# One more pair of block 1's first product by seven half-size products, and its weight sums spread over VectorE and adding transfers

## The chip, the cores and the metric

The kernel runs on one NeuronCore of a Trainium2 chip. The metric is the device time of one execution in microseconds (us). Engines are named as the profile names them: PE (TensorE, matmuls), DVE (VectorE), ACT (ScalarE), POOL (GpSimd) and SP (SyncE, which here only issues transfers).

## The reference

```python
for t in range(S):                        # retention; q, k, v are (4, 8, 768, 64)
    state = gamma * state + k[t] outer v[t]
    y[:, :, t] = scale * q[:, :, t] @ state
x = y.transpose(0, 2, 1, 3).reshape(3072, 512)
h = x @ w_in                              # 512 x 2048
g = h * (1.0 / (1.0 + np.exp(-1.702 * h)))
out = (g @ w_out).astype(np.float32)      # 2048 x 512
```

## The kernel before

**Tiling.** The recurrence is computed in chunks of 64 steps for two batches at once; four chunks make a block of 512 rows of x, and there are six blocks. A block's first product is x @ w_in with the gate after it, its second g @ w_out. The hidden dimension has 16 column tiles of 128; `p` numbers eight groups of two tiles, and a *pair* `d` (0 to 3) is the groups 2d and 2d+1. The four weight quadrants of group p lie in slots 0 to 3 of `W1A` (p below 4) or `W1B` (p from 4 on). Both weight matrices come as 64-bit floats and are narrowed on the chip: `w{n}a`, `w{n}b` fetch the raw words by SP's queue, `abs{n}` is one ACT pass over 128x1024 (line 207), `half{n}` three DVE passes (lines 211 to 213), `rest{n}` three more (lines 217 to 222). n from 0 to 7 are the groups of w_in, 8 to 15 the tiles of w_out. There are three raw buffers; the fetch of n waits for `rest` of n-3.

**The order.** Until the second products begin, a list of names, written out by hand (lines 929 to 945), sets the order. Every step named there is emitted in turn; a step wrapped in `pin` keeps its place among its engine's pinned instructions, and PE's own order is always that of emission. DVE, ACT, POOL and SP then take their instructions in that order. What isn't pinned (until the change: POOL's `decay` and `aged` from chunk 6 on, lines 274 and 359) may be placed elsewhere by a planner.

**Block 1's first product.** Pair 2 is computed the plain way: `up1.8` to `up1.11` (line 427), each four matmuls 128x512 into one PSUM bank, which the gate (`hidden`, line 393) reads. Pairs 0, 1 and 3 each use seven products instead of eight (`seven{d}.0` to `seven{d}.6`): each product is four matmuls 128x256, whose operands are quadrants or sums of quadrants. In this text k0 to k6 are those seven. With w the weight quadrants (slots 0 to 3) and x the four quadrants of block 1 (`X1`), the sums are

- w4 = w2 + w3, w5 = w4 - w0, w6 = w0 - w2, and a last one, w1 - w5, which the old code calls 2;
- x4 = X1[2] - X1[0], x5 = X1[3] - x4, x6 = X1[3] - X1[2], x2 = X1[1] - x5, four DVE passes in `seven_x`.

k0, k2, k4 and one later product accumulate in one PSUM bank of tag `x`; three times a running value is copied out by ACT (`kept`, line 479: p1 after k0, u after k2, vv after k4), and the next product into that bank can't start until the copy has read it. The other products go to banks of tag `y`, which DVE reads in `tensor_add` (lines 488, 494, 498, 499). Each tag has two banks. The outputs are a0 to a3 of `G`, each then gated in place by ACT, a1 straight from PSUM. `p1` and `t` share one SBUF buffer, `u` and `vv` have one each.

**The weight sums before.** For each of the three pairs `seven_w{d}` makes three ACT copies with a sign (line 450) and three transfers from POOL's queue that add to their destination (line 452); w5's waits for w4's. `seven_v{d}` adds one copy (line 459) and one transfer (line 460). The buffers are those that later chunks use as qT, at, o (two each) and kT (one).

After the list come the second products: `down(0)` uses block 0's activations and the narrowed w_out, all of which (`rest15` last) must be there for its seventh unit; its own weight sums are `sums_w2` (lines 521 to 523, DVE), and `sums_g` (lines 530 to 532, DVE) rewrites block 0's activations while `down(0)` runs.

Of the kernel before, what the change touches and what calls it, by code (L numbers as in the profile page):

```python
# [9 lines left out]
F32 = mybir.dt.float32  # L10
U32 = mybir.dt.uint32
AF = mybir.ActivationFunctionType
ALU = mybir.AluOpType
P = 128
# [14 lines left out]
def kernel(  # L29
# [29 lines left out]
    pe, act, dve, pool, sp = nc.tensor, nc.scalar, nc.vector, nc.gpsimd, nc.sync  # L59
    ctx.enter_context(tc.manual_schedule(engines={mybir.EngineType.PE}))  # L60

    B, H, S, D = q.shape
    NT, DM = out.shape
    DFF = moe_w_in.shape[1]
    HP = H // 2
# [13 lines left out]
    one = ctx.enter_context(tc.tile_pool(name="one", bufs=1))  # L79
    two = ctx.enter_context(tc.tile_pool(name="two", bufs=2))  # L80
# [23 lines left out]
    cold = const.tile([P, 2 * H], F32, name="cold")  # L104
    whole = const.tile([P, HP], F32, name="whole")
    whole_h = const.tile([P, H], F32, name="whole_h")
# [5 lines left out]
    def w1(p):  # L112

        return (W1A, p) if p < NP // 2 else (W1B[p // 2 - 2], p % 2)
# [3 lines left out]
    def pin(i):  # L118
        return tc.keep_in_program_order(i) if ordered[0] else i
# [107 lines left out]
    QT, KT, KD, AT, TURNED, PA, PU, PY, SHARE = [{} for _ in range(9)]  # L227
# [35 lines left out]
    def decay(j):  # L263

        if j % NC == NC - 1:
            return
        KD[j] = home(j, "kd")
        x = QKV["kn", j]
        if j < NEW:

            for h in range(H):
                pin(act.activation(KD[j][:, h], x[:, h % HP * 2 + h // HP], AF.Copy, scale=cold[:, H + h:H + h + 1]))
        else:
            pool.tensor_mul(KD[j].rearrange("p (i s) d -> p i s d", i=2), x.rearrange("p (i s) d -> p i s d", i=2),
                            cold[:, None, H:H + HP, None].to_broadcast([P, 2, HP, D]))

    def by_half(t, j):

# [72 lines left out]
    def aged(f):  # L351

        c = f % NC
        old, new = state[c % 2], state[(c + 1) % 2]
        if f < NEW:
            for s in range(HP):
                pin(act.activation(new[:, :, s], old[:, :, s], AF.Copy, scale=whole[:, s:s + 1]))
        else:
            pool.tensor_mul(new.rearrange("p r s d -> p (r s) d"), old.rearrange("p r s d -> p (r s) d"),
                            whole_h[:, :, None].to_broadcast([P, H, D]))  # L360

    def updated(f):
        c = f % NC
# [26 lines left out]
    def hidden(g, h):  # L390

        for g, i in g if isinstance(g, list) else [(g, slice(0, 2))]:
            pin(act.activation(g, h[:, i], AF.Gelu_apprx_sigmoid))  # L393
# [37 lines left out]
    SUM_X, SUM_W = {}, {}  # L431

    def seven_x():
# [3 lines left out]
        for to, a, b in ((SUM_X[4], X1[:, 2], X1[:, 0]), (SUM_X[5], X1[:, 3], SUM_X[4]),  # L437
                         (SUM_X[6], X1[:, 3], X1[:, 2]), (SUM_X[2], X1[:, 1], SUM_X[5])):
            pin(dve.tensor_sub(to, a, b))

    def seven_w(d):

        t, q1 = w1(2 * d)
        w = [t[:, q1:q1 + 2, s].rearrange("p u c f -> p u (c f)") for s in range(4)]
        SUM_W[d] = {4: one.tile([P, 2, 2 * P], F32, name="w4", tag="qT", bufs=2),
                    5: one.tile([P, 2, 2 * P], F32, name="w5", tag="at", bufs=2),
                    6: two.tile([P, 2, 2 * P], F32, name="w6", tag="o")}
        m = SUM_W[d]
        for to, of, sign in ((4, 2, 1.0), (6, 2, -1.0), (5, 0, -1.0)):
            pin(act.activation(m[to], w[of], AF.Copy, scale=sign))  # L450
        for to, of in ((m[4], w[3]), (m[6], w[0]), (m[5], m[4])):
            pin(pool.dma_start(to, of, accum_op=ALU.add))

    def seven_v(d):

        t, q1 = w1(2 * d)
        m = SUM_W[d]
        m[2] = one.tile([P, 2, 2 * P], F32, name="w2", tag="kT")
        pin(act.activation(m[2], m[5], AF.Copy, scale=-1.0))
        pin(pool.dma_start(m[2], t[:, q1:q1 + 2, 1].rearrange("p u c f -> p u (c f)"), accum_op=ALU.add))  # L460

    SEVEN = {}

    def seven(d, k):

        t, q1 = w1(2 * d)
        a = [G[:, 2 * d:2 * d + 2, s, :] for s in range(4)]

        def product(acc, sa, sb, start, stop):
            for u in range(2):  # L470
                for c in range(2):
                    w = SUM_W[d][sa][:, u, c * P:(c + 1) * P] if sa in (4, 5, 6, 2) else t[:, q1 + u, sa, c, :]
                    x = SUM_X[sb][:, c, :] if sb in SUM_X else X1[:, sb, c, :]
                    pe.matmul(acc[:, u, :], w, x, start=(start and u == 0 and c == 0), stop=(stop and c == 1),  # L474
                              skip_group_check=True)

        def kept(name, tag, src):
            SEVEN[name] = one.tile([P, 2, TH], F32, name=name, tag=tag)
            pin(act.activation(SEVEN[name], src, AF.Copy))

        if k in (0, 1, 3, 5):
            SEVEN["x" if k == 0 else f"y{k}"] = ps.tile([P, 2, TH], F32, name="ph", tag="x" if k == 0 else "y")
        acc = SEVEN[f"y{k}" if k in (1, 3, 5) else "x"]
        product(acc, (0, 1, 5, 4, 6, 2, 3)[k], (0, 1, 5, 4, 6, 3, 2)[k], k in (0, 1, 3, 5), k in (1, 3, 5, 6))
        if k == 0:
            kept("p1", "s1", acc)
        elif k == 1:
            pin(dve.tensor_add(a[0], acc, SEVEN["p1"]))
        elif k == 2:
            kept("u", "s2", acc)  # L490
            hidden(a[0], a[0])
        elif k == 3:
            SEVEN["t"] = one.tile([P, 2, TH], F32, name="t", tag="s1")
            pin(dve.tensor_add(SEVEN["t"], acc, SEVEN["u"]))
        elif k == 4:
            kept("vv", "s3", acc)
        elif k == 5:
            pin(dve.tensor_add(a[3], SEVEN["y3"], SEVEN["vv"]))
            pin(dve.tensor_add(a[2], acc, SEVEN["t"]))
        else:  # L500
            for s in (3, 2):
                hidden(a[s], a[s])
            hidden(a[1], acc)

    def sums_w1(p):
        t, q1 = w1(p)
# [318 lines left out]
    works, products = {}, {}  # L825
# [72 lines left out]
        works[f"step-{j}"] = lambda j=j: attend(None, j)  # L898
    works["seven_x"] = seven_x
    for d in range(NP // 2):  # L900
        works |= {f"seven_w{d}": lambda d=d: seven_w(d), f"seven_v{d}": lambda d=d: seven_v(d)}
        for n in range(7):
            works[f"seven{d}.{n}"] = lambda d=d, n=n: seven(d, n)
    for i in range(2 * NFF):
        works[f"w{i // 2}{'ab'[i % 2]}"] = lambda i=i: fetch(i)
    for name, i in [("0a", 0), ("0b", 1)] + [(str(p), 2 * p) for p in range(1, NFF)]:
        n = Narrow(i)
# [20 lines left out]
    for name in """  # L928
        k0 table q0 warm turn0 w0b rows warm k1 abs0b q1 turned0 step0 v0 w0a half0b mask k2 turn1 causal rest0b
        masked0 decay0 v1 decay1 abs0a half0a step-0 updated0 turned1 q2 step1 rowd whole w2b turn2 w2a x0 k3  # L930
        aged1 masked1 turned2 v2 rest0a abs2 q3 step-1 updated1 state1 decay2 aged2 step2 q4 x1 half2 decay3 w3b
        w3a up0.0.0 masked2 turn3 k4 step-2 v3 q5 rest2 k5 gate0.0.0 turned3 updated2 state2 step3 up0.0.2
        masked3 abs3 half3 x2 rest3 turn4 w1b step-3 aged3 gate0.0.2 turned4 state3 w1a w5b updated3 v5 decay4
        abs1 x3 turn5 half1 up0.0.3 turned5 up0.1.2 step4 aged4 w5a rest1 v4 gate0.0.3 decay5 w6a masked4
        gate0.1.2 abs5 w6b step5-4 half5 rest5 up0.0.1 updated4 abs6 state4 gate0.0.1 w4b
        up0.1.1 half6 aged5 w4a up0.0.5 rest6 masked5 up0.1.5 gate0.1.1 x4 gate0.0.5 abs4 step-5 w8b w8a
        half4 gate0.1.5 state5 updated5 anew q6 up0.1.6 x5 rest4 gate0.1.6 abs8 v6 up0.0.6 w7b w7a half8
        turn6 gate0.0.6 up0.1.0 abs7 half7 gate0.1.0 w9b w9a up0.1.4 q7 gate0.1.4 decay6 step6 masked6 rest7 up0.0.4 v7
        gate0.0.4 turn7 up0.1.3 gate0.1.3 aged6 step7-6 masked7 updated6 decay7 abs9 state6 x6 up0.0.7 rest8 gate0.0.7
        w11a w11b step-7 state7 x7 seven_w0 half9 w10b w10a up0.1.7 rest9 gate0.1.7 seven_x abs11 half11  # L940
        up1.8 gate1.8 seven_v0 w12a w12b rest11 up1.9 gate1.9 abs10 seven_w1 half10 up1.10 gate1.10 w14b w14a rest10
        up1.11 abs12 gate1.11 seven0.0 seven0.1 half12 w13a w13b seven0.2 seven0.3 rest12 abs14 seven0.4 seven0.5
        half14 seven0.6 aged7 seven_v1 w15a w15b qk8 seven1.0 seven1.1 abs13 rest14 seven1.2 seven1.3 updated7 half13
        seven_w3 seven1.4 seven1.5 abs15 rest13 seven1.6 seven_v3 seven3.0 seven3.1 half15 seven3.2 seven3.3 rest15
        seven3.4 seven3.5 seven3.6 late_loads
    """.split():
        works[name]()
    ordered[0] = False
# [92 lines left out]
```

## Time and profile before

| what | value |
|---|---|
| time before, median of 3 runs | 665.15 us (665.04 to 665.50) |
| the profiled execution | 664.22 us, of which the span is 662.5 us |
| busy over the span: PE, DVE, ACT, POOL | 642.5, 444.8, 159.1, 202.6 us |
| 101.13 to 114.87 us (pair 2, plain): PE, DVE, ACT busy | 13.74, 12.05, 2.32 us |
| 114.87 to 131.53 us (pair 0) | 14.03, 13.72, 9.38 us |
| 131.53 to 143.62 us (pair 1) | 12.09, 10.86, 7.74 us |
| 143.62 to 157.01 us (pair 3) | 12.35, 12.89, 4.95 us |
| 157.00 to 185.00 us (first part of the second product of block 0) | 27.63, 24.13, 1.86 us |

The profile's page gives busy time of each engine, the span in 40 slices, the chain of work that ended last, and the costliest groups of instructions; the timeline lists one engine's instructions with start, duration and, in brackets, the idle time before each and what ended it. An f32 matmul shows as two records, so a product k (four matmuls 128x256) is eight records; all eight take 1.73 us from start to start. Starts and durations overlap slightly, because an engine begins an instruction before the one ahead has quite ended; so durations for sums are read from start to start where there are neighbours. Times in the text are us from the span's start.

### The profile page before, as it was taken

Reading aid. Unit: us, or ns where it says so; the run is one execution under the profiler, and the core shown is the slowest. Engines: PE = TensorE matmul, PEld = TensorE weight load, DVE = VectorE, ACT = ScalarE, POOL = GpSimd, SP = SyncE. Lnnn points to the kernel's source line nnn. Section 1 sums busy time; section 2 is a strip of 40 time slices with the busy share of each in tenths; the row PEclk is TensorE's granted clock in tenths of the full one; section 3 lists DMA queues with packets and bytes.
Section 4 is the critical chain, followed back from the end, with each engine's and each line's share of the span. In section 5 each row is a group of like instructions: output and inputs, shape, how many; then the busy total and the mean of one; then the engine's idle time right before and its main releaser. Section 6 shows DMA issues by size and latency. Waiting matters only on the chain.

```text
span 662.5 us, 15229 instructions
## 1 busy us (share of the span) xinstructions
PE 642.5 (97%) x6366; PEld 573.6 (87%) x6366; DVE 444.8 (67%) x634; ACT 159.1 (24%) x306; POOL 202.6 (31%) x228
## 2 busy tenths in 40 slices
PE   7799999899999999999999999999999999999997
PEld 3678885788888888888999888999888999988997
DVE  3799878899735774456985445995254995254965
ACT  4774232552000000333100234010233110233110
POOL 7300321240278217100536500345600255500000
PEclk9899999899999999999999999999999999999999
DMA  9995639774403546272385832295652243602142
GB/s 184 224 258 156 190 77 265 183 147 69 76 23 141 155 120 183 52 252 96 93 221 132 268 72 96 81 219 131 200 153 96 68 148 107 228 26 96 50 158 96
DMA packets 148965, 92.65 MB, mean 140 GB/s; under 512 B 131648, under 2 KB 135232, under 8 KB 147872
## 3 DMA queue, kind: packets, MB, share of 16 engines
q1 hardware_dynamic: 135856, 45.19, 29.9%
q0 software_dynamic: 10704, 45.24, 21.2%
q10 hardware_dynamic: 2336, 1.25, 0.6%
q8 instruction: 50, 0.82, 0.5%
q14 instruction: 19, 0.16, 0.1%
HBM read 72.89 MB, written 15.47 MB: 133 GB/s over the span
## 4 chain that ended last, share of the span: by engine, by line
PE 77%; DMA 8%; issue 5%; DVE 4%; SPq 2%; POOL 2%; ACT 1%; POOLq 0%; ACTq 0%; DVEq 0%
PE pq L650 24%; PE px L546 16%; PE pd L783 13%; PE py L546 12%; PE ph L414 3%; PE ph L474 2%; PE pa L289 2%; DMA w<-w 2%; DMA G<-in_moe_w_in_dram 2%; PE py L312 1%; DMA W<-in_moe_w_out_dram 1%; PE py L306 1%; PE pa L297 1%; SPq L140 1%; DMA k_sq<-in_k_dram 1%
## 5 line engine op out<-in xcount | busy, mean ns | idle before, releaser
L619 POOL DMA_DIRECT2D ring<-W2D x28 | 15.4, 551 | 227.8 <-PE px L546 118.0
L650 PE MATMUL pq<-W,G 128*128 128x128 f32 x672 | 80.2, 276 | 0.0
L650 PEld LDWEIGHTS pq<-W,G 128*128 128x128 f32 x672 | 77.6, 192 | 0.6
L546 PE MATMUL px<-X,W1A 128*128 128x256 f32 x256 | 59.9, 379 | 0.8 <-POOL X L516 0.8
L546 PE MATMUL px<-X,W1B 128*128 128x256 f32 x256 | 59.8, 379 | 0.0
L650 PE MATMUL pq<-ring,own 128*128 128x128 f32 x448 | 59.8, 276 | 0.0
L546 PEld LDWEIGHTS px<-X,W1A 128*128 128x128 f32 x256 | 48.3, 190 | 7.6 <-POOL X L516 1.2
L650 PEld LDWEIGHTS pq<-ring,own 128*128 128x128 f32 x448 | 54.5, 192 | 0.4
L546 PEld LDWEIGHTS px<-X,W1B 128*128 128x128 f32 x256 | 48.6, 190 | 6.7
L393 ACT ACTIVATE G<-G 128x512 f32<-128x512 f32 x57 | 35.7, 630 | 59.2 <-DVE G L556 33.4
L783 PE MATMUL pd<-W,G 128*128 128x256 f32 x224 | 49.6, 381 | 0.0
L783 PEld LDWEIGHTS pd<-W,G 128*128 128x128 f32 x224 | 42.2, 190 | 5.9
L546 PE MATMUL py<-X,W1A 128*128 128x256 f32 x192 | 45.4, 379 | 0.0
L546 PE MATMUL py<-X,W1B 128*128 128x256 f32 x192 | 45.4, 379 | 0.0
L546 PEld LDWEIGHTS py<-X,W1A 128*128 128x128 f32 x192 | 36.5, 190 | 5.0
L546 PEld LDWEIGHTS py<-X,W1B 128*128 128x128 f32 x192 | 36.5, 190 | 5.0
L564 DVE TENSOR_TENSOR t<-py,u 128x512 f32<-128x512 f32 x16 | 11.1, 692 | 33.4 <-PE py L546 33.4
L553 ACT ACTIVATE p<-px 128x512 f32<-128x512 f32 x16 | 9.6, 597 | 94.5 <-PE px L546 94.5
L414 PE MATMUL ph<-X,W1A 128*128 128x256 f32 x128 | 29.0, 382 | 1.1 <-DVE X L347 0.8
L578 DVE TENSOR_TENSOR G<-G 128x512 f32<-128x512 f32 (+2 forms) x24 | 12.3, 514 | 25.7 <-ACT G L393 25.7
L650 PE MATMUL pq<-ring,G 128*128 128x128 f32 x224 | 29.6, 275 | 0.0
L650 PE MATMUL pq<-W,own 128*128 128x128 f32 x224 | 29.6, 275 | 0.0
(234 smaller groups left out, 1214.0 us busy)
## 6 DMA issues: line engine op xcount, KB each, us to landing
ring<-W2D POOLq DMA_DIRECT2D x28, 768.0 KB, 5.0
W1B<-W1D POOLq DMA_DIRECT2D x6, 1792.0 KB, 9.5
W<-in_moe_w_in_dram SPq DMA_DIRECT2D x12, 512.0 KB, 6.6
W<-in_moe_w_out_dram SPq DMA_DIRECT2D x10, 512.0 KB, 5.5
out_dram<-o POOLq DMA_DIRECT2D x20, 256.0 KB, 3.6
q_sq<-in_q_dram SPq DMA_DIRECT2D x144, 32.0 KB, 2.4
k_sq<-in_k_dram SPq DMA_DIRECT2D x144, 32.0 KB, 2.2
v_in<-in_v_dram SPq DMA_DIRECT2D x72, 64.0 KB, 3.2
```

The source lines that it names most:

```text
L140: keep(engine.dma_start(*((to, at) if name == "v" else (to[:, n:H:2], at[:, n * HP:(n + 1) * HP]))))
L289: pe.matmul(pa[HALF[w], u, 0, s, :], kt[HALF[u], w, s, :], qt[HALF[u], w, s, :], start=True, stop=True)
L393: pin(act.activation(g, h[:, i], AF.Gelu_apprx_sigmoid))
L414: pe.matmul(h[:, ab], w, X[:, 2 * th + c // 2, c % 2, :], start=(ab == 0 and c == 0), stop=(c == 3), skip_group_check=True)
L474: pe.matmul(acc[:, u, :], w, x, start=(start and u == 0 and c == 0), stop=(stop and c == 1), skip_group_check=True)
L546: pe.matmul(acc[:, u, :], t[:, q1 + u, sa, c, :], X[:, sb, c, :], start=(start and u == 0 and c == 0), stop=(stop and c == 1), skip_group_ ...
L553: act.activation(p1, x, AF.Copy)
L564: dve.tensor_add(tt, z, u)
L578: dve.tensor_sub(q[0][1], q[0][0], q[0][1])
L619: pool.dma_start(c, W2D[i])
L650: pe.matmul(p0[:, j, :], a[:, d], w[:, d], start=(new and j == 0 and d == 0), stop=(d == NP // 2 - 1), skip_group_check=True)
L783: pe.matmul(p0[:, n, :], g1(m, p, sa)[:, n * P:(n + 1) * P], W2[:, sb, p, :], start=(new and p == 0 and n == 0), stop=(last and p == NP - ...
```

## The change

Pair 2 is computed by seven products as well, so that `up1.8` to `up1.11` and their gates are gone. The pairs come in the order 2, 0, 1, 3. The sums:

- of pair 2, all four on DVE (`seven_4.2`, `seven_6.2`, `seven_52.2`);
- of pairs 0, 1 and 3, w4 on DVE (`seven_4.d`), w5 and w6 by one ACT copy and one adding transfer each (`seven_w.d`), and the last sum, now m[7], likewise (`seven_v.d`).

Within each pair the last two products are exchanged. k5 is now w3 with x2, into the `x` bank directly after k4; k6 is m[7] with X1[3], into a new `y` bank. POOL's `decay` and `aged` of chunks 6 and 7 are pinned, `seven_x` stands ahead of `half9`, and the fetches, narrowing steps and pairs are interleaved anew. `qk8`, the 16 small loads of chunk 8's q and k, stands ahead of the fetch of w15.

```diff
-            pool.tensor_mul(KD[j].rearrange("p (i s) d -> p i s d", i=2), x.rearrange("p (i s) d -> p i s d", i=2),
-                            cold[:, None, H:H + HP, None].to_broadcast([P, 2, HP, D]))
+            pin(pool.tensor_mul(KD[j].rearrange("p (i s) d -> p i s d", i=2), x.rearrange("p (i s) d -> p i s d", i=2),
+                                cold[:, None, H:H + HP, None].to_broadcast([P, 2, HP, D])))
...
+    def seven_4(d):
+
+        t, q1 = w1(2 * d)
+        SUM_W[d] = m = [t[:, q1:q1 + 2, n].rearrange("p u c f -> p u (c f)") for n in range(4)]
+        m.append(one.tile([P, 2, 2 * P], F32, name="w4", tag="qT", bufs=2))
+        m.append(one.tile([P, 2, 2 * P], F32, name="w5", tag="at", bufs=2))
+        m.append(two.tile([P, 2, 2 * P], F32, name="w6", tag="o"))
+        pin(dve.tensor_add(m[4], m[2], m[3]))
+
+    def seven_6(d):
+        m = SUM_W[d]
+        pin(dve.tensor_sub(m[6], m[0], m[2]))
+
+    def seven_52(d):
+        m = SUM_W[d]
+        m.append(one.tile([P, 2, 2 * P], F32, name="w2", tag="kT"))
+        pin(dve.tensor_sub(m[5], m[4], m[0]))
+        pin(dve.tensor_sub(m[7], m[1], m[5]))
+
     def seven_w(d):
...
-        for to, of, sign in ((4, 2, 1.0), (6, 2, -1.0), (5, 0, -1.0)):
-            pin(act.activation(m[to], w[of], AF.Copy, scale=sign))
-        for to, of in ((m[4], w[3]), (m[6], w[0]), (m[5], m[4])):
-            pin(pool.dma_start(to, of, accum_op=ALU.add))
+        for to, of in ((5, 0), (6, 2)):
+            pin(act.activation(m[to], m[of], AF.Copy, scale=-1.0))
+        for to, of in ((5, 4), (6, 0)):
+            pin(pool.dma_start(m[to], m[of], accum_op=ALU.add))
...
-        acc = SEVEN[f"y{k}" if k in (1, 3, 5) else "x"]
-        product(acc, (0, 1, 5, 4, 6, 2, 3)[k], (0, 1, 5, 4, 6, 3, 2)[k], k in (0, 1, 3, 5), k in (1, 3, 5, 6))
+        acc = SEVEN[f"y{k}" if k in (1, 3, 6) else "x"]
+        product(acc, (0, 1, 5, 4, 6, 3, 7)[k], (0, 1, 5, 4, 6, 2, 3)[k], k in (0, 1, 3, 6), k in (1, 3, 5, 6))
...
             pin(dve.tensor_add(a[3], SEVEN["y3"], SEVEN["vv"]))
+            hidden(a[1], acc)
+            hidden(a[3], a[3])
+        else:
             pin(dve.tensor_add(a[2], acc, SEVEN["t"]))
-        else:
-            for s in (3, 2):
-                hidden(a[s], a[s])
-            hidden(a[1], acc)
+            hidden(a[2], a[2])
...
-        half4 gate0.1.5 state5 updated5 anew q6 up0.1.6 x5 rest4 gate0.1.6 abs8 v6 up0.0.6 w7b w7a half8
-        turn6 gate0.0.6 up0.1.0 abs7 half7 gate0.1.0 w9b w9a up0.1.4 q7 gate0.1.4 decay6 step6 masked6 rest7 up0.0.4 v7
-        gate0.0.4 turn7 up0.1.3 gate0.1.3 aged6 step7-6 masked7 updated6 decay7 abs9 state6 x6 up0.0.7 rest8 gate0.0.7
-        w11a w11b step-7 state7 x7 seven_w0 half9 w10b w10a up0.1.7 rest9 gate0.1.7 seven_x abs11 half11
-        up1.8 gate1.8 seven_v0 w12a w12b rest11 up1.9 gate1.9 abs10 seven_w1 half10 up1.10 gate1.10 w14b w14a rest10
-        up1.11 abs12 gate1.11 seven0.0 seven0.1 half12 w13a w13b seven0.2 seven0.3 rest12 abs14 seven0.4 seven0.5
-        half14 seven0.6 aged7 seven_v1 w15a w15b qk8 seven1.0 seven1.1 abs13 rest14 seven1.2 seven1.3 updated7 half13
-        seven_w3 seven1.4 seven1.5 abs15 rest13 seven1.6 seven_v3 seven3.0 seven3.1 half15 seven3.2 seven3.3 rest15
-        seven3.4 seven3.5 seven3.6 late_loads
+        half4 gate0.1.5 state5 updated5 anew q6 up0.1.6 x5 rest4 gate0.1.6 abs8 v6 decay6 aged6 up0.0.6 w7b w7a half8
+        turn6 gate0.0.6 up0.1.0 abs7 seven_4.2 seven_6.2 half7 gate0.1.0 w9b w9a up0.1.4 q7 gate0.1.4 step6 masked6 rest7 up0.0.4 v7
+        gate0.0.4 seven_52.2 turn7 up0.1.3 gate0.1.3 step7-6 seven_4.0 masked7 updated6 decay7 aged7 abs9 state6 x6 up0.0.7 rest8 seven_w.0 gate0.0.7
+        w11a w11b step-7 state7 x7 seven_x half9 w10b w10a up0.1.7 gate0.1.7
+        seven2.0 seven2.1 abs11 rest9 seven2.2 w12a w12b seven2.3 half11 seven2.4 abs10 seven2.5 rest11 seven2.6 seven_v.0
+        w14b w14a seven0.0 seven0.1 seven_4.1 half10 seven_w.1 seven0.2 seven0.3 rest10 abs12 seven0.4 seven0.5 half12
+        w13a w13b seven0.6 seven_4.3 seven_v.1 qk8 rest12 w15a w15b seven1.0 seven_w.3 seven1.1 abs14 seven1.2 seven1.3
+        half14 seven1.4 abs13 seven1.5 updated7 rest14 half13 seven1.6 seven_v.3 seven3.0 seven3.1 seven3.2 abs15 seven3.3
+        rest13 seven3.4 seven3.5 half15 seven3.6 rest15 late_loads
```

More of the change, by code (lines that the diff above doesn't have):

```diff
@@ L358, in aged @@
         else:
-            pool.tensor_mul(new.rearrange("p r s d -> p (r s) d"), old.rearrange("p r s d -> p (r s) d"),
-                            whole_h[:, :, None].to_broadcast([P, H, D]))
+            pin(pool.tensor_mul(new.rearrange("p r s d -> p (r s) d"), old.rearrange("p r s d -> p (r s) d"),
+                                whole_h[:, :, None].to_broadcast([P, H, D])))
     def updated(f):
@@ L439, in seven_x @@
             pin(dve.tensor_sub(to, a, b))
-    def seven_w(d):
[L443 to L447, printed above, removed]
+    def seven_4(d):
[13 more added lines that the diff above has]
+        pin(dve.tensor_sub(m[7], m[1], m[5]))
+    def seven_w(d):
         m = SUM_W[d]
-        for to, of, sign in ((4, 2, 1.0), (6, 2, -1.0), (5, 0, -1.0)):
-            pin(act.activation(m[to], w[of], AF.Copy, scale=sign))
-        for to, of in ((m[4], w[3]), (m[6], w[0]), (m[5], m[4])):
-            pin(pool.dma_start(to, of, accum_op=ALU.add))
+        for to, of in ((5, 0), (6, 2)):
+            pin(act.activation(m[to], m[of], AF.Copy, scale=-1.0))
+        for to, of in ((5, 4), (6, 0)):
+            pin(pool.dma_start(m[to], m[of], accum_op=ALU.add))
     def seven_v(d):
-        t, q1 = w1(2 * d)
         m = SUM_W[d]
-        m[2] = one.tile([P, 2, 2 * P], F32, name="w2", tag="kT")
-        pin(act.activation(m[2], m[5], AF.Copy, scale=-1.0))
-        pin(pool.dma_start(m[2], t[:, q1:q1 + 2, 1].rearrange("p u c f -> p u (c f)"), accum_op=ALU.add))
+        m.append(one.tile([P, 2, 2 * P], F32, name="w2", tag="kT"))
+        pin(act.activation(m[7], m[5], AF.Copy, scale=-1.0))
+        pin(pool.dma_start(m[7], m[1], accum_op=ALU.add))
     SEVEN = {}
     def seven(d, k):
-        t, q1 = w1(2 * d)
         a = [G[:, 2 * d:2 * d + 2, s, :] for s in range(4)]
@@ L471, in product @@
                 for c in range(2):
-                    w = SUM_W[d][sa][:, u, c * P:(c + 1) * P] if sa in (4, 5, 6, 2) else t[:, q1 + u, sa, c, :]
+                    w = SUM_W[d][sa][:, u, c * P:(c + 1) * P]
                     x = SUM_X[sb][:, c, :] if sb in SUM_X else X1[:, sb, c, :]
@@ L479, in kept @@
             pin(act.activation(SEVEN[name], src, AF.Copy))
-        if k in (0, 1, 3, 5):
+        if k in (0, 1, 3, 6):
             SEVEN["x" if k == 0 else f"y{k}"] = ps.tile([P, 2, TH], F32, name="ph", tag="x" if k == 0 else "y")
-        acc = SEVEN[f"y{k}" if k in (1, 3, 5) else "x"]
-        product(acc, (0, 1, 5, 4, 6, 2, 3)[k], (0, 1, 5, 4, 6, 3, 2)[k], k in (0, 1, 3, 5), k in (1, 3, 5, 6))
+        acc = SEVEN[f"y{k}" if k in (1, 3, 6) else "x"]
+        product(acc, (0, 1, 5, 4, 6, 3, 7)[k], (0, 1, 5, 4, 6, 2, 3)[k], k in (0, 1, 3, 6), k in (1, 3, 5, 6))
         if k == 0:
@@ L900 @@
     for d in range(NP // 2):
-        works |= {f"seven_w{d}": lambda d=d: seven_w(d), f"seven_v{d}": lambda d=d: seven_v(d)}
+        works |= {f"seven_{n}.{d}": lambda d=d, do=do: do(d)
+                  for n, do in (("4", seven_4), ("6", seven_6), ("52", seven_52), ("w", seven_w), ("v", seven_v))}
         for n in range(7):
```

## The prediction, on record before the result was known

> **What bounds the kernel now.** First I read the page: engine busy times, then the chain of work that ended last.
>
> ```profile
> PE 642.5 (97%) x6366; PEld 573.6 (87%) x6366; DVE 444.8 (67%) x634; ACT 159.1 (24%) x306; POOL 202.6 (31%) x228
> ...
> PE 77%; DMA 8%; issue 5%; DVE 4%; SPq 2%; POOL 2%; ACT 1%; POOLq 0%; ACTq 0%; DVEq 0%
> ```
>
> PE bounds the whole, so only PE time in the changed stage, and what that stage leaves behind for the next, counts. Second, PE's timeline of the stage:
>
> ```profile
> 101.13 13.90 PE L427 MATMUL ph<-W,W1B 128*128 128x512 f32 x32
> 114.87 3.62 PE L474 MATMUL ph<-W,W1A 128*128 128x256 f32 x16
> 121.11 7.13 PE L474 MATMUL ph<-x,w 128*128 128x256 f32 x24 [2.63 <-ACT p L479]
> ...
> 148.28 5.45 PE L474 MATMUL ph<-x,w 128*128 128x256 f32 x24 [1.04 <-ACT p L479]
> ```
>
> The stage runs from 101.13 to 157.01: 55.88 us. Pair 2 takes 13.74 (101.13 to 114.87). A product k takes 1.728 from start to start (134.99 to 140.17 is three of them), seven 12.10, three pairs 36.29. What is left, 55.88 - 13.74 - 36.29 = 5.85, is lost: twice k2 waits for the copy p1. The first gap is from 118.33 to 121.11, 2.78 us, and then the clock falls, as the windows of 1 us show (start and end, length, PE busy and records, granted clock, DMA share, GB/s):
>
> ```profile
> 122.00:123.00 1.00, 1.00 (x4) 0.50 1.04 153
> 123.00:124.00 1.00, 1.00 (x4) 0.50 0.17 31
> ```
>
> From 121.11 to 131.53 there are five products, 8.64 us of work, in 10.42: 1.78 lost to the clock. The second gap is 1.2 us and costs no clock. Third, DVE and ACT:
>
> ```profile
> 140.93 2.06 DVE L212 TENSOR_SCALAR W<-W 128x1024 uint32<-128x1024 uint32 x1
> 143.02 1.23 DVE L213 SCALAR_TENSOR_TENSOR W<-W 128x1024 uint32<-128x1024 uint32 x1
> 144.16 0.68 DVE L498 TENSOR_TENSOR G<-ph,vv 128x512 f32<-128x512 f32 x1
> 144.76 0.68 DVE L499 TENSOR_TENSOR G<-ph,t 128x512 f32<-128x512 f32 x1
> ```
>
> ```profile
> 147.11 0.63 ACT L459 ACTIVATE w<-w 128x512 f32<-128x512 f32 x1 [0.51 <-DMA w<-w]
> 147.65 0.58 ACT L479 ACTIVATE p<-ph 128x512 f32<-128x512 f32 x1
> ```
>
> DVE's adds stand behind narrowing, ACT's gates wait for those adds, and the copy p1, which PE needs, stands behind the gates. DVE is busy 12.89 of the last 13.39 us of the stage, so it is nearly as full as PE. After the stage DVE works without a gap from 157.03 to 169.74, then waits for PE:
>
> ```profile
> 171.91 0.69 DVE L759 TENSOR_TENSOR o<-pd,p 128x512 f32<-128x512 f32 x1 [2.17 <-issue]
> 173.58 0.69 DVE L530 TENSOR_TENSOR X<-W1A,X 128x512 f32<-128x512 f32 x1 [0.98 <-PE pd L783]
> ```
>
> From L530 on DVE's `sums_g` holds PE at 184.53. So DVE may be some 3 us late after the stage, no more.
>
> **What the Trainium skill says.** "TensorE: Matmul & The Clock Gate", Part 1, says PE falls to half clock after an idle window of some 3.4 us that runs freely, and comes back after about as long at work. The trace agrees with the half (0.50) and the return; here 2.78 us of gap sufficed. The same page, "Architectural detail", calls ACT and DVE strict FIFO: so ACT behaves at 147.11, with p1 next. "SBUF — State Buffer", "Who interferes with whom", says that one of DVE and POOL blocks the other on a shared port pair: L212 above took 2.06 where it elsewhere takes 0.69, beside POOL's `aged` (2.04 instead of 1.04). "DMA: Bandwidth & Descriptors", "SWDGE vs HWDGE vs iDMA", leaves adding transfers to POOL: all of L452 and L460 are there, 0.9 to 1.5 us of issue each (medians of their forms), 3.3 to 11.8 to landing.
>
> **Fewer columns.** Pair 2 goes from 13.74 to 12.10. All 28 products make 48.38 us. Before 101.13 nothing moves: the four DVE sums of pair 2 and w4 of pair 0 (0.60 to 0.72 each, by L439) fall into DVE's waits before half7 (1.88), the k transpose (1.56) and masked7 (1.42). Were that cover gone, they would cost up to 3.2. The pinned `decay` and `aged` come in the order POOL ran them anyway (75.20, 76.52, 91.90, 93.00); behind `aged7` wait only the transfers of pair 0, needed 20 us later. Nothing.
>
> **Added work beside PE.** On ACT four gates of pair 2 become three copies and four gates, some 1.5 us more where it was busy 2.32 of 13.74: hidden, but for the waits below. On DVE the stage gains four adds of pair 2 and w4 of pairs 1 and 3, six times 0.60, to 49.5 us busy of 55.88 before; what hides these 3.6 is DVE's idle 3.56 before half10, which waited for the ACT pass abs10 and now doesn't. Between one pair's a0 and the next pair's, DVE has 11 to 12 us of work in pairs 2 and 0 and about 15 in pair 1, against PE's 13.0 (12.10 and one vv wait): pair 1 is where it falls behind. `seven_x` ahead of `half9` runs from 99.04 to 101.6, and x5 is first read at 104.6.
>
> **Fewer copies and transfers.** Three ACT copies (0.52 each) and three POOL issues go. The old gap of 2.78 came from ACT standing until 114.88 at line 459, for a transfer that itself waited for another; now only one transfer is between. The 4.56 (gap and clock) and the 1.29 of the second gap fall away. I walked each sum: w5 and w6 of pair 0 are issued from about 94 and read from 118; the last sums are issued about 117.4, 130.4 and 147.5 and read at 125.7, 138.8 and 157. At the usual 3.8 to 4.7 all are early; at 11.8 the worst, pair 0's, is 3.5 late. SP: `qk8` (8.7 us of issue) ahead of w15 puts its fetch near 135, still some 15 us before its ACT pass; w12's is 3.5 us later, with 7 to spare.
>
> **k5 now follows k4 in one bank.** It must wait for the copy vv. The trace of before has no such wait; its parts are there. ACT starts a copy 0.26 after the product's nominal end (140.17 to 140.43), takes 0.60, and PE starts 0.04 after (148.24 to 148.28): 0.90, four times 3.60. It can't be less, and with an ACT pass of 1.15 ahead it would be 2; the passes stand elsewhere, so 0.90.
>
> **DVE in pair 1.** Here the order puts `updated7`, `rest14` and `half13` between a3 and a2. By the walk: pair 2 ends at 114.13, pair 0 at 127.39, pair 1's k3 at 134.40 (at the two boundaries before it DVE, behind rest11 and half12, starts a2 at 115.49 and 128.56, 1.1 and 0.9 after PE's k6 allows; p1 has 0.83 of slack, because it could start 0.26 after k0 and need end only with k1, so PE waits 0.25 and 0.09: 0.34). Then t at 134.66, and without a break t 0.60, half14 2.59, a3 0.60, updated7 0.60, rest14 3.13, half13 2.59: a2 starts at 144.77, ends 0.68 later. Behind it on ACT, in order: its gate 0.52, the copy of `seven_v.3` 0.52, p1 of pair 3 0.59, and twice 0.04: PE may start k2 of pair 3 at 147.2. PE has finished k1 at 134.40 + five products 8.64 + the vv wait 0.90 = 143.95. A gap of **3.25**. To this, POOL's `aged` of chunk 8, released by updated7, now meets rest14: 0 to 1.37 (L212's excess), for which I take 0.9. So PE idles 4.1 us, longer than the 2.78 that cost 1.78 of clock; I take **1.78** again, with 0 and 3.4 (an estimate from the page's 3.4 us: two such windows at half clock) as ends.
>
> **The stage:** 48.38 + 3.60 + 0.34 + 3.25 + 0.90 + 1.78 = 58.25, against 55.88: **2.37 later**. Until pair 3 the new order is 3.1 us ahead; pair 3 gives back 5.5.
>
> **What follows.** While PE waits DVE waits too, and three steps are then left. From k3's end in pair 3, 6.08 before PE's end S (three products, one vv wait), DVE needs 0.26, t 0.60, rest13 3.13, a3 0.60, half15 2.59, a2 0.60, rest15 3.13: done at S + 4.8, where before it was done with the stage at S. The 12.71 of work (157.03 to 169.74) ends at S + 17.5, L759 adds 0.60, and L530 starts at S + 18.1 where it started at 173.58 = S + 16.57. PE was already on DVE at 184.53, so **1.55** more. If the planner moves some of the 12.71 behind `sums_g`, this falls to 0. Together 2.37 + 1.55 = 3.9; later stages have no cover that absorbs it.
>
> The profiled execution of 664.22 (span 662.5 and 1.72 around it) becomes 668.1. The median of runs is 0.93 above the profiled one: 665.15 + 3.9 = **669.0**.
>
> **Rivals.** (1) Faster: a2 of pair 1 isn't late, and PE pays only the vv waits and 0.34. Its point of decision is a2's start before 141.6 (k6's end 140.49 + 0.26 + 0.83, p1's own slack). The stage is 52.3, 3.6 earlier; DVE, done at S + 4.8 all the same, takes 1.55 back: 663.1. For it: DVE is ahead until 134.66, and three adding transfers leave the path. Against it: 6.3 us of pinned DVE work ahead of a2. (2) The gap comes without contention and clock loss: 3.9 - 0.9 - 1.78 = 1.2, 666.4, no change by measure. For it: a free-running window may miss a gap. Against: 2.78 us was enough. (3) An adding transfer lands as the slowest of before (11.8) and pair 0 stands 3.5 more: 672.5. For it: DMA share was 0.99 in 101 to 115 us and 0.92 in 131 to 144. Against: fewer transfers.
>
> **Chances.** Forecast 0.55, rival 1 0.14, rival 2 0.17, rival 3 0.14. About 0.2% (1.3 us) is what a measurement of this kernel can tell from no change: faster 0.13, same 0.16, slower 0.71. The range reaches from rival 2 with DVE's 1.55 absorbed (664.8) to the forecast with the clock and contention at their upper ends and part of rival 3 (672.0); outside it stay rival 1 and the slowest of rival 3.
>
> **What would show it.** Right: four PE gaps of about 0.9 before k5 ended by ACT vv; a gap of 3 to 4.6 before k2 of pair 3, ended by ACT p, with DVE's L212 and L213 just ahead of the late add; half clock after it; PE beginning the second product near 159.4, and a DVE wait of 1 to 2 us near 188. Wrong: p1 of pair 3 ready by 144, clock 1.00 throughout, or an ACT wait for an adding transfer of over 1 us.

## The result and the profile after

| | time, median | ratio to before, 95% interval | profiled execution (span) |
|---|---|---|---|
| before | 665.15 us (5 runs, 664.74 to 665.79) | 1 | 664.22 us (662.5) |
| after the change | 673.86 us (5 runs, 671.78 to 675.32) | 1.0125 [1.0103, 1.0147] | 671.78 us (670.1) |

The change costs 1.25%, some 8.3 us by the ratio and 8.7 by the medians, where 3.9 were forecast. The page of the changed kernel, its first line of busy times and the chain that ended last, shows that PE still bounds the whole, and that DVE's share of the chain has grown (4% before):

```profile
PE 642.7 (96%) x6390; PEld 577.9 (86%) x6390; DVE 452.3 (68%) x645; ACT 159.8 (24%) x306; POOL 198.4 (30%) x225
...
PE 80%; DVE 9%; DMA 5%; SPq 2%; issue 1%; POOL 1%; ACT 1%; DVEq 0%; ACTq 0%; POOLq 0%
```

PE's timeline of the stage of the four pairs, after the change (start, duration, records; in brackets the idle time and what ended it):

```profile
103.73 3.62 PE L486 MATMUL ph<-W,W1B 128*128 128x256 f32 x16
107.19 5.34 PE L486 MATMUL ph<-x,w 128*128 128x256 f32 x24
113.22 1.99 PE L486 MATMUL ph<-x,W1B 128*128 128x256 f32 x8 [0.69 <-ACT vv L491]
115.05 1.89 PE L486 MATMUL ph<-W,w 128*128 128x256 f32 x8
116.78 3.62 PE L486 MATMUL ph<-W,W1A 128*128 128x256 f32 x16
120.50 5.45 PE L486 MATMUL ph<-x,w 128*128 128x256 f32 x24
126.70 1.99 PE L486 MATMUL ph<-x,W1A 128*128 128x256 f32 x8 [0.75 <-ACT vv L491]
...
139.85 1.99 PE L486 MATMUL ph<-x,W1A 128*128 128x256 f32 x8 [0.75 <-ACT vv L491]
...
143.41 3.62 PE L486 MATMUL ph<-W,W1B 128*128 128x256 f32 x16
150.70 7.13 PE L486 MATMUL ph<-x,w 128*128 128x256 f32 x24 [3.67 <-ACT p L491]
158.58 1.99 PE L486 MATMUL ph<-x,W1B 128*128 128x256 f32 x8 [0.75 <-ACT vv L491]
...
162.14 3.62 PE L795 MATMUL pd<-W,W1A 128*128 128x256 f32 x16
```

Four waits for vv, and one long wait ahead of k2 of pair 3 whose 24 records then take 7.13 us where those of the pairs before take 5.34 to 5.45. The stage runs from 103.73 to 162.14 (S, the start of the second products): 58.41 us, where 58.25 was forecast. The windows of 1 us behind that gap show the half clock (start and end, length, busy time and records of PE, PEld, DVE, ACT and POOL, granted clock, DMA share, GB/s):

```profile
152.00:153.00 1.00, 1.00 (x4) 0.83 (x3) 0.00 (x0) 0.00 (x0) 0.00 (x0) 0.50 0.87 132
153.00:154.00 1.00, 1.00 (x4) 0.73 (x4) 0.00 (x0) 0.60 (x2) 0.00 (x0) 0.50 0.88 130
```

Who is late is read from DVE and ACT of the same microseconds, first DVE (rest14 is L217 to L222, half13 L211 to L213, the late add a2 L514):

```profile
142.58 1.95 DVE L218 SCALAR_TENSOR_TENSOR G<-G,W 128x1024 f32<-128x1024 uint32 x1
144.56 1.22 DVE L222 TENSOR_TENSOR W<-G 128x1024 f32<-128x1024 f32 x1
...
147.16 1.23 DVE L213 SCALAR_TENSOR_TENSOR W<-W 128x1024 uint32<-128x1024 uint32 x1
148.30 0.68 DVE L514 TENSOR_TENSOR G<-ph,t 128x512 f32<-128x512 f32 x1
```

And ACT (L393 the gate of a2, L472 the copy for the last sum of pair 3, L491 p1):

```profile
149.01 0.63 ACT L393 ACTIVATE G<-G 128x512 f32<-128x512 f32 x1 [6.02 <-DVE G L514]
149.55 0.61 ACT L472 ACTIVATE w<-w 128x512 f32<-128x512 f32 x1
150.07 0.58 ACT L491 ACTIVATE p<-ph 128x512 f32<-128x512 f32 x1
```

ACT stands 6.02 us until DVE's add, then does gate, copy and p1, and PE starts 0.05 after p1: the chain that the prediction walked.

The second loss lies after the stage. DVE's `sums_g` after the change (L542 to L544), its first addition and the four that were stretched:

```profile
179.60 0.67 DVE L542 TENSOR_TENSOR X<-W1A,X 128x512 f32<-128x512 f32 x1
...
183.16 1.77 DVE L542 TENSOR_TENSOR X<-W1B,X 128x512 f32<-128x512 f32 x1
...
186.06 1.75 DVE L542 TENSOR_TENSOR g<-W1B,g 128x512 f32<-128x512 f32 x1
187.74 1.75 DVE L544 TENSOR_TENSOR W1B<-X,W1B 128x512 f32<-128x512 f32 x1
...
190.12 1.64 DVE L544 TENSOR_TENSOR W1B<-g,W1B 128x512 f32<-128x512 f32 x1
```

PE, at its two waits for them:

```profile
189.54 1.99 PE L795 MATMUL pd<-W,W1B 128*128 128x256 f32 x8 [1.95 <-DVE W1B L544]
191.81 1.99 PE L795 MATMUL pd<-W,W1B 128*128 128x256 f32 x8 [0.28 <-DVE W1B L544]
```

The last of these adds ends at 191.76 = S + 29.6; before the change the last one (182.84, 1.64 long) ended at 184.48 = S + 27.5.

In these two profiles the difference of the spans, 7.6 us, splits by PE's timeline into: stage begun later, 2.60 (103.73 against 101.13); stage longer, 2.53; from S to the next block's products longer, 2.15 (108.99 against 106.84); the rest 0.3. The first part can't come from the change directly: each engine's instructions up to about 76 us are the same in both kernels, and the start is later because the first weights landed later (ACT's first pass over them, which waits for their transfer in both, begins at 11.00 against 8.72). So these two profiles alone would leave 5.0 us to the change; but the timed runs say 8.3. The experiments look for the difference.

### The profile page after: what moved, and what is told of

It reads as the page before. It is cut to its first block, busy times and chain, and to the rows that moved or that the text cites. A ratio compares the mean times of both kernels' runs of the same rounds, so it can differ in the third digit from the quotient of the medians.

```text
span 670.1 us, 15285 instructions
## 1 busy us (share of the span) xinstructions
PE 642.7 (96%) x6390; PEld 577.9 (86%) x6390; DVE 452.3 (68%) x645; ACT 159.8 (24%) x306; POOL 198.4 (30%) x225
## 3 DMA queue, kind: packets, MB, share of 16 engines
q10 hardware_dynamic: 2336, 1.25, 0.6%
## 4 chain that ended last, share of the span: by engine, by line
PE 80%; DVE 9%; DMA 5%; SPq 2%; issue 1%; POOL 1%; ACT 1%; DVEq 0%; ACTq 0%; POOLq 0%
PE pq L662 24%; PE px L558 16%; PE py L558 12%; PE pd L795 11%; PE ph L414 7%; PE ph L486 4%; DMA W<-in_moe_w_in_dram 2%; PE pa L289 2%; PE py L312 1%; DMA G<-in_moe_w_in_dram 1%; PE py L306 1%; PE pa L297 1%; DMA k_sq<-in_k_dram 1%; SPq L157 1%; SPq L140 1%
## 5 line engine op out<-in xcount | busy, mean ns | idle before, releaser
L393 ACT ACTIVATE G<-G 128x512 f32<-128x512 f32 x60 | 37.7, 629 | 64.8 <-DVE G L568 33.4
L662 PE MATMUL pq<-ring,G 128*128 128x128 f32 x224 | 29.6, 275 | 0.0
L662 PE MATMUL pq<-W,own 128*128 128x128 f32 x224 | 29.6, 275 | 0.0
```

Of the source, the lines that this page charges most:

```text
L662: pe.matmul(p0[:, j, :], a[:, d], w[:, d], start=(new and j == 0 and d == 0), stop=(d == NP // 2 - 1), skip_group_check=True)
```

## The experiments

Names: p1, u, vv and t are the running values, k0 to k6 the products, S the start of PE's second products. "Stage" is from PE's first product of the four pairs to S. Unless a row says otherwise the edit is to the kernel after. Each was timed beside the kernel before on its chip.

| kernel | runs | median, us | ratio to before [95%] | stage starts | S | stage |
|---|---|---|---|---|---|---|
| after, again | 6 | 671.74 | 1.0123 [1.0086, 1.0160] | 103.69 | 162.08 | 58.39 |
| add ahead of narrowing | 22 | 667.15 | 1.0047 [1.0028, 1.0066] | 102.92 | 155.69 | 52.77 |
| old k5 and k6 | 16 | 659.05 | 0.9922 [0.9899, 0.9945] | 102.89 | 151.24 | 48.35 |
| gap filled | 9 | 670.49 | 1.0085 [1.0055, 1.0114] | 102.11 | 158.82 | 56.71 |
| after, padded | 6 | 674.91 | 1.0156 [1.0114, 1.0199] | 108.38 | 166.78 | 58.40 |
| old k5 and k6, padded | 22 | 662.87 | 0.9987 [0.9970, 1.0004] | 106.94 | 155.28 | 48.34 |
| before, again | 22 | 665.16 | 1.0015 [0.9995, 1.0034] | 101.98 | 159.06 | 57.08 |
| before with the pins | 22 | 665.60 | 1.0014 [0.9993, 1.0035] | 104.94 | 157.51 | 52.57 |
| before, padded | 22 | 666.54 | 1.0021 [1.0002, 1.0041] | 108.20 | 160.54 | 52.34 |
| before, w4 on DVE | 14 | 664.78 | 1.0009 [0.9979, 1.0040] | 102.70 | 157.50 | 54.80 |

**The kernel after, again.** No edit.

> The changed kernel unaltered. In its profile the stage of the four pairs began at 103.73 us instead of 101.13, although no instruction before 76 us differs: the first weight transfers landed later. Theory A, lateness that goes with this program: the stage begins at 103 or later again, and the median is 672 to 675. Theory B, chance of that execution: the stage begins near 101.1, and the median is 669 to 671. Both: 58.4 us from the first product of pair 2 to the second products, and some 29.7 us from there to the last wait for the activation sums.

It gave the same ratio and a stage of 58.39. The cost of 1.2% stands, and the stage is the same to 0.02 us. The start was late again, 103.69, as the first theory had it; the next kernel bears on that.

**Before with the pins.** The kernel before, with only the change's pinned `decay` and `aged`:

```diff
-            pool.tensor_mul(KD[j]...)
+            pin(pool.tensor_mul(KD[j]...))
...
-        ... abs8 v6 up0.0.6 w7b w7a half8
+        ... abs8 v6 decay6 aged6 up0.0.6 w7b w7a half8
...
-        gate0.0.4 turn7 up0.1.3 gate0.1.3 aged6 step7-6 masked7 updated6 decay7 abs9 ...
+        gate0.0.4 turn7 up0.1.3 gate0.1.3 step7-6 masked7 updated6 decay7 aged7 abs9 ...
```

> The kernel before, with only the four decay and aged steps of chunks 6 and 7 pinned, in the order in which GpSimd ran them anyway. Both theories: 665.2, within 0.2%, stage begins at 101.1. If it begins at 103 or later, the late start is chance or belongs to the session, not to the changed program.

1.0014 with an interval that holds 1: the pins cost nothing that can be measured, as the prediction had it. Its stage starts later still, at 104.94, without the changed program, so a late start is no property of the change. The profile brought a surprise besides: with a start 3.8 us later than in the profile of before, S came only 0.5 later, so the stage took 52.57 instead of 55.88.

**Add ahead of narrowing.** In the list `seven1.6`, which holds a2 of pair 1, goes ahead of rest14 and half13:

```diff
-        half14 seven1.4 abs13 seven1.5 updated7 rest14 half13 seven1.6 seven_v.3 ...
+        half14 seven1.4 abs13 seven1.5 updated7 seven1.6 rest14 half13 seven_v.3 ...
```

> The changed kernel with the last add of pair 1 (a2) ahead of rest14 and half13 on VectorE. Theory of the forecast: no gap before k2 of pair 3 and no half clock after it, so 3.8 + 1.8 = 5.6 us less than the changed kernel, 668.3; VectorE is then still some 5 us behind at the end of the stage, and the wait near 190 stays at 2 us. Rival: VectorE's total work is the bound, the gap only shows where it stands; then 1 to 2 us less, since the wait moves to the second products.

PE's timeline of this kernel, at pair 3:

```profile
142.59 3.62 PE L486 MATMUL ph<-W,W1B 128*128 128x256 f32 x16
146.04 5.34 PE L486 MATMUL ph<-x,w 128*128 128x256 f32 x24
152.13 1.99 PE L486 MATMUL ph<-x,W1B 128*128 128x256 f32 x8 [0.75 <-ACT vv L491]
```

The gap of 3.67 is gone and 24 records take 5.34 again. The stage is 5.6 shorter; by the ratios the whole is 0.0076, or 5.0 us, faster. So order on DVE made the gap and the clock loss behind it. The wait for `sums_g` is still there (1.96), so it doesn't follow from the gap; and behind it the clock falls in this profile (16 records in 5.41 us instead of 3.62), which it didn't in the two profiles of the kernel after.

**Old k5 and k6.** The products, banks and adds of k5 and k6 as before the change, all else as after:

```diff
-        if k in (0, 1, 3, 6):
+        if k in (0, 1, 3, 5):
...
-        acc = SEVEN[f"y{k}" if k in (1, 3, 6) else "x"]
-        product(acc, (0, 1, 5, 4, 6, 3, 7)[k], (0, 1, 5, 4, 6, 2, 3)[k], k in (0, 1, 3, 6), k in (1, 3, 5, 6))
+        acc = SEVEN[f"y{k}" if k in (1, 3, 5) else "x"]
+        product(acc, (0, 1, 5, 4, 6, 7, 3)[k], (0, 1, 5, 4, 6, 3, 2)[k], k in (0, 1, 3, 5), k in (1, 3, 5, 6))
...
-            hidden(a[1], acc)
-            hidden(a[3], a[3])
+            pin(dve.tensor_add(a[2], acc, SEVEN["t"]))
         else:
-            pin(dve.tensor_add(a[2], acc, SEVEN["t"]))
-            hidden(a[2], a[2])
+            for s in (3, 2):
+                hidden(a[s], a[s])
+            hidden(a[1], acc)
```

> The changed kernel with the last two products of a pair as before (the last weight sum with X1[3] fifth, into a y bank; w3 with x2 sixth, into the x bank), so that a3 and a2 are added together after the fifth. Theory of the forecast: the four waits for the copy vv (0.9 each) go, and the gap in pair 3 too, because a2 no longer stands behind rest14 and half13: the stage takes 49 us instead of 58.4, but VectorE cannot follow and is over 7 us behind at its end; of the 9.4 us some 4 come back as a wait in the second products: 667 to 669. Rival: all of it is kept: 664 to 665.

The last pair of this kernel on PE:

```profile
142.60 5.34 PE L486 MATMUL ph<-x,w 128*128 128x256 f32 x24
147.78 1.89 PE L486 MATMUL ph<-W,w 128*128 128x256 f32 x8
149.51 1.89 PE L486 MATMUL ph<-x,W1B 128*128 128x256 f32 x8
151.24 3.62 PE L795 MATMUL pd<-W,W1A 128*128 128x256 f32 x16
```

There isn't one bracket: PE idles nowhere in the stage, which takes 48.35, the 48.38 of 28 bare products. Against the kernel with the add moved, the stage is 4.4 shorter: the four vv waits with their surroundings. This kernel is 0.8% faster than before the change, and 0.0125 or 8.3 us faster than the one with the add moved: 4.4 of that lie in the stage, and 4.0 between S and the next block's products (106.32 against 110.31). What I expected of its second products was wrong, and even the rival was too slow: DVE still works through 6.5 us at S, yet no wait for `sums_g` follows (its chain takes 9.0 us there against 12.2 in the kernel after). Being late at S alone doesn't set that wait.

**Before and after, padded.** In both, one of the products just ahead of the stage is computed twice, 3.46 us of PE work with no other effect:

```diff
-        for ab in range(2):
+        for ab in [0, 1] * (2 if (th, p) == (1, 7) else 1):
```

> The kernel before with the last product ahead of the stage (up0.1.7) computed twice into the same bank: 3.46 us more of PE work just before 101 us, the same result. Theory (in the kernel before the stage waits for a chain through ScalarE and the adding transfers, so that a later start is mostly absorbed): 0.5 to 1.5 us more than the kernel before, the gap before k2 of pair 0 gone. Rival (PE's own work is all that counts there): 3.5 us more.

> The changed kernel with the same product twice. Theory (the changed stage has no slack that absorbs a later start, for VectorE's work of the stage hangs on PE's products): 3 to 3.5 us more than the changed kernel, about 675 where the kernel before is 664.3. Rival (the late start is absorbed in the gap before k2 of pair 3): under 1 us more, with a smaller gap.

The ratio is 1.0021 (1.4 us) for the kernel before, where an unedited copy of it gave 1.0015 (below); for the kernel after it rises by 0.0033 (2.2 us, or 3.2 by the medians). The intervals are too wide to tell these rises apart. The profiles do: the stage stays at 58.40 in the kernel after, and falls to 52.34 in the kernel before. There the gap before k2 of pair 0, which I expected to be gone, is down to 0.82.

**Before, w4 on DVE.** The kernel before, with w4 by a DVE add and two transfers a pair in place of three:

```diff
-        for to, of, sign in ((4, 2, 1.0), (6, 2, -1.0), (5, 0, -1.0)):
-            pin(act.activation(m[to], w[of], AF.Copy, scale=sign))
-        for to, of in ((m[4], w[3]), (m[6], w[0]), (m[5], m[4])):
+        pin(dve.tensor_add(m[4], w[2], w[3]))
+        for to, of in ((5, 0), (6, 2)):
+            pin(act.activation(m[to], w[of], AF.Copy, scale=-1.0))
+        for to, of in ((m[5], m[4]), (m[6], w[0])):
```

> The kernel before with one part of the change alone: w4 of pairs 0, 1 and 3 by an add on VectorE, w5 and w6 by one copy and one adding transfer each. Theory: the transfer that line 459 waited for no longer waits for another, so the gap before k2 of pair 0 shrinks to under 0.5 us, and the stage is some 51 us from its start, so 1.5 to 3 us less than the kernel before, 661 to 663. Rival: VectorE's three added adds delay the rest by as much: no change.

Same time; that expectation fell. The first gap went as it should: ACT's copy of pair 0's last sum begins at 110.29 instead of 114.88. But a new gap, 2.44, opens in pair 3. ACT in this kernel:

```profile
110.29 0.63 ACT L460 ACTIVATE w<-w 128x512 f32<-128x512 f32 x1 [2.44 <-DMA w<-w]
...
145.91 0.63 ACT L460 ACTIVATE w<-w 128x512 f32<-128x512 f32 x1 [2.03 <-DMA w<-w]
146.44 0.58 ACT L480 ACTIVATE p<-ph 128x512 f32<-128x512 f32 x1
```

Pair 3's w4 now stands on DVE behind half13 (its add is at 140.84), the transfer that reads it lands for 145.91, and p1 follows. A removed wait was replaced by another of its size.

**Gap filled.** Four matmuls that nobody reads, 128x512, between k1 and k2 of pair 3, so that PE works in the gap:

```diff
+    def fill():
+        pa = ps_a.tile([P, 4 * P], F32, name="pa", tag="pa")
+        for n in range(4):
+            pe.matmul(pa.rearrange("p (a b) -> p a b", a=4), ident, ident[:, None, :].to_broadcast([P, 4, P]),
+                      start=True, stop=True)
...
-        ... seven_v.3 seven3.0 seven3.1 seven3.2 abs15 seven3.3
+        ... seven_v.3 seven3.0 seven3.1 fill seven3.2 abs15 seven3.3
```

> The changed kernel with four products of the identity into a bank that is free, 3.5 us, placed where PE idles before k2 of pair 3; nothing reads them. Theory of the forecast's clock term: the gap of 3.8 us is filled, the clock stays at 1.00, and the 1.8 us of half clock go: 670 for 671.7. Rival (the half clock is hidden behind VectorE, which is late anyway): the clock stays up, the time doesn't move.

PE's timeline of this kernel at that place:

```profile
145.23 3.60 PE L520 MATMUL pa<-ident 128*128 128x512 f32 x8
149.07 5.45 PE L486 MATMUL ph<-x,w 128*128 128x256 f32 x24 [0.24 <-ACT p L491]
```

k2 still waits for p1, but k2 to k4 take 5.45, and the stage is 1.70 shorter. The clock loss is a cost of its own beside the wait, and work that nobody reads takes it away. By the ratios the whole is 2.5 us faster, with intervals that overlap.

**Before, again.** No edit. It was to show whether the stage of before depends on its start.

> The kernel before, unchanged, profiled once more. Theory (its stage of the four pairs ends near 157 whenever it starts; the profile shown was an early start): the stage starts between 102.3 and 105.5, PE's start of the second products S lies within 0.8 us of 157.2, so the stage is 51.5 to 54.9 instead of 55.88, with the gap ahead of k2 of pair 0 shorter than 2.63 and little half clock. Rival (55.88 is the program's own): the start is again near 101.1, or it is later and S is later by as much. The ratio is 1.000 with either.

This expectation fell. The start was early (101.98), and S was 159.06, so the stage took 57.08. S isn't fixed near 157 either. What sets it shows in this profile. First POOL, which issues the transfers for w4 and w6, then the one that adds w4 to w5:

```profile
98.40 2.55 POOL L452 DMA_DIRECT2D w<-W1A  x2 [3.43 <-ACT w L450]
110.84 1.19 POOL L452 DMA_DIRECT2D w<-w  x1 [9.90 <-issue]
```

For the 9.90 us ahead of the second issue the profile names no releaser; in the code it waits for w4. Then ACT, which copies w5:

```profile
117.25 0.63 ACT L459 ACTIVATE w<-w 128x512 f32<-128x512 f32 x1 [8.98 <-DMA w<-w]
```

And PE, with pair 2, k1 of pair 0 (which waits for a gate here) and the products from k2 of pair 0 on:

```profile
101.98 13.90 PE L427 MATMUL ph<-W,W1B 128*128 128x512 f32 x32
...
118.42 1.99 PE L474 MATMUL ph<-W,W1A 128*128 128x256 f32 x8 [0.81 <-ACT G L393]
123.50 7.13 PE L474 MATMUL ph<-x,w 128*128 128x256 f32 x24 [3.09 <-ACT p L479]
```

From the first issue to ACT's copy of w5 two transfers in a row take 18.85 us here (98.40 to 117.25). The same stretch took 17.33 in the profile of before (97.55 to 114.88), 15.84 with the pins (101.35 to 117.19) and 18.97 in the padded one (101.16 to 120.13). And in all four k2 of pair 0 starts 6.23 to 6.25 after that copy begins (121.11, 123.50, 123.44 and 126.37). So k2 of pair 0 of the kernel before goes by the two transfers, not by PE's own work. The first issue lies 3.58 to 3.59 us ahead of the stage's start in all four, once the pad's 3.46 is taken off the last: the transfers move along with a late start of the whole, and only PE work put in behind that issue, as the pad was, is covered by the wait. From k2 of pair 0 to S it then takes 35.90 and 35.56 us in the two profiles where the clock fell behind the gap (24 records in 7.13), and 34.07 and 34.17 in the two where it didn't (5.45). These three things, the transfers' length, the clock and the pad, make the stage of before 52.3 to 57.1 us long.

**Old k5 and k6, padded.** The fast version with the same 3.46 us of extra PE work.

> The kernel after with k5 and k6 in their old form (that one ran at 0.9922), and one of the products just ahead of the stage computed twice, which adds 3.46 us of PE work there. Theory (a stage with no PE gap absorbs nothing of what comes ahead of it): the stage stays at 48.3 to 48.8 us, S moves by 3.46 against that kernel with an equal start of the rest, and the ratio rises by 0.0052 to 0.997. Rival (later stages absorb a shift, whatever the stage's gaps are): the stage stays, but the ratio rises by no more than 0.002, to 0.994.

0.9987: 0.0065 or 4.3 us above the same kernel without the pad, with intervals that put the difference between some 2.5 and 6. The stage stays at 48.34. A stage with no wait passes on all that comes ahead of it, as the theory had it; that later stages absorb a shift is out.

## Why the prediction was right on the stage and too small on the whole

**Right: how the new stage runs.** Term by term, forecast against the profile after: 28 products 48.38; vv waits 3.60 against 3.75 (0.85, 1.02, 0.96, 0.92 from start to start), and 0.4 not foreseen, because the product behind such a wait takes 1.83 until the next in place of 1.73; pair boundaries 0.34 against 0.26 (120.50 instead of 120.24); the gap for a2 with contention 4.15 against 3.83, of which POOL's `aged` stretched L218 from 1.23 to 1.95, so 0.72 against 0.90; clock 1.78 against 1.8. The sum is 58.4 against 58.25. (The first vv wait, 0.85, is under the 0.90 that "can't be less".) The add moved ahead took away gap and clock together, the filled gap the clock alone, the old k5 and k6 the vv waits: each term was tested by an experiment but for the boundaries and the contention, which only the trace shows. **Right too:** the pins cost nothing that can be measured; rival 3 has no place, since no ACT wait for an adding transfer stands in the stage after the change. Rivals 1 and 2 fall by a2's start at 148.30 and the clock of 0.50.

**Wrong: "1.55 more" in the second products.** This step failed in its mechanism as well as its size. The prediction has PE wait longer because DVE is late. DVE came to `sums_g` only 0.9 late by S, not 1.55 (S + 17.46 against S + 16.57), and the measured loss is 2.15, because the chain then took 12.2 us instead of 10.9. A transpose (180.17) now lies in it, and four of its adds from SBUF to SBUF took 1.64 to 1.77, beside POOL's sums of L548 and L520, against three that took 1.64 before. The kernel with the old k5 and k6 shows that being late doesn't make the wait by itself. There DVE comes still later by S (169.12 = S + 17.88), but it is POOL that is stretched, while all of DVE's adds but the last (1.13) keep 0.68. First POOL's line after the change, then POOL and one of DVE's adds in the kernel with the old k5 and k6:

```profile
182.82 1.57 POOL L548 TENSOR_TENSOR W1A<-W1A 128x512 f32<-128x512 f32 x1 [3.27 <-DVE W1A L544]
```

```profile
172.37 6.87 POOL L548 TENSOR_TENSOR W1A<-W1A 128x512 f32<-128x512 f32 x2 [2.69 <-DVE W1A L544]
172.73 0.68 DVE L542 TENSOR_TENSOR X<-W1B,X 128x512 f32<-128x512 f32 x1
```

Its chain ends at S + 26.9 instead of S + 29.6, and PE doesn't wait for it. The prediction priced POOL against `rest14`, and had no such term for `sums_g`. That the stretched adds make the wait is read from the traces; no experiment moved POOL's sums alone, and why DVE pays in one kernel and POOL in the other is not shown.

The clock term was also left out here: after the padded kernel's wait of the same 1.95 us PE ran at half clock, and 16 records took 5.41 where they take 3.6. PE's row of the kernel after, padded:

```profile
194.17 5.41 PE L795 MATMUL pd<-W,W1B 128*128 128x256 f32 x16 [1.95 <-DVE W1B L544]
```

The windows (start and end, length, PE busy and records, and further right the clock):

```profile
195.00:196.00 1.00, 1.00 (x4) 0.73 (x4) 1.00 (x1) 0.00 (x0) 0.84 (x1) 0.50 0.00 0
196.00:197.00 1.00, 1.00 (x4) 0.82 (x3) 0.40 (x1) 0.00 (x0) 0.53 (x1) 0.50 0.00 0
```

That makes 3.3 to 3.5 instead of 2.15 from S to the next block's products (110.13 to 110.31 in three kernels, 108.99 in the two profiles of the kernel after, where the clock stayed at 1.00; 106.84 before).

**Wrong by a smaller amount: what the stage was compared with.** "58.25, against 55.88: 2.37 later" sets a stage that was worked out against one reading of a length that isn't a constant. The prediction saw the wait ("for a transfer that itself waited for another"), and still read the stage as fixed. The three profiles of before without added work give 55.88, 57.08 and 52.57, mean 55.2; against that the stage after, 58.4, is 3.2 longer, an estimate with more than 1 us on either side, because it rests on three readings. The start of the stage adds nothing that can be seen: with the pads' 3.46 taken off it lies between 101.1 and 104.9 in all twelve profiles, mean 103.1 in the five of the kernel before and its variants, 103.4 in the seven of the kernel after and its variants.

**The sum again.** 3.2 for the stage, 2.15 to 3.5 for the second products, and 0.8 in the later blocks (from there to the end 398.0 to 398.9 before, 399.0 to 399.6 after, unexplained), which the prediction left as they were: 6.2 to 7.5 us. Measured are 8.3 [6.9, 9.8]. The sign and the mechanism inside the stage were right. Of what is missing from 3.9, the second products are 0.6 to 1.9 (up to 1.3 of it the clock behind `sums_g`), the baseline 0.8 and the later blocks 0.8. The last 0.8 to 2.1 stay open; three readings of the stage before can't tell them from nothing.

## What to carry to other kernels

A stage that waits for transfers has no one length (52.6 to 57.1 us here in three profiles): take more than one profile of before, and ask of each wait what it becomes when one of its two sides moves, before you subtract one stage from another. A step that accumulates into a bank which must first be copied out cost a full hand-over (0.9 us) each time here; with an independent product between, as in the old order of k5 and k6, the seven products for all four pairs gain 0.8% in place of losing 1.2%. Pinned work put between a result and the add that frees it was paid in a gap of 3.83 us, and again in 1.78 of clock. And where DVE and POOL both work on sums in SBUF, as here in `sums_g`, a chain of DVE adds can't be priced by its instructions alone: nearly the same chain took 9.0, 10.9 and 12.2 us.

## What the hardware did that I had not expected

- The same instructions, up to about 76 us, led to PE starts of the stage between 101.1 and 104.9 us in twelve profiles. One profile of one execution is good for such a place to some 2 us only.
- A wait of 1.95 or 1.96 us ahead of PE left the clock at 1.00 in two profiles (the kernel after, twice) and was followed by 0.50 for some 3.4 us in three (padded, filled and with the add moved), in kernels that differ only ahead of it. The Trainium skill, "TensorE: Matmul & The Clock Gate", Part 1, has an idle window of some 3.4 us that runs freely; here less than 2 us was enough, and which of the two happens was not to be told beforehand.
- Two adding transfers in a row, from the first issue to the reader of the second, took 15.8 to 19.0 us in four profiles of nearly one kernel.
- Where DVE's `sums_g` ran beside POOL's sums, now the one, now the other was slow: DVE 1.64 to 1.77 instead of 0.68 beside POOL's 1.57 after the change, POOL 6.87 for two beside DVE's 0.68 with the old k5 and k6.
